# A pair's row sums one slot sooner, and one addition moved among four subtractions

## The chip, the cores and the metric

The kernel runs on one core of a Trainium2 chip. A core has five engines that run side by side, each with its own queue of instructions in a fixed order: TensorE (PE in the profile; its weight loads are listed as PEld), VectorE (DVE), ScalarE (ACT), GpSimd (POOL) and SyncE (SP), which here issues the DMA transfers. They meet through semaphores: an instruction that needs another engine's result waits at the head of its queue, and everything behind it waits too.

The metric is the time of one execution in device microseconds. Before the change it was 1029.43 us, the median of three runs (1029.31 to 1030.74).

## The reference

Two blocks follow each other. The first is block-sparse attention for a batch of 4, 8 heads, 768 tokens and head dimension 64:

```
scores = scale * q @ k.T
scores = where(mask, scores, -1e9)      # blocks of 32: window, first and last block, 3 sampled blocks
attn   = exp(scores - max) / (sum + 1e-9)
x      = attn @ v                       # -> (4, 768, 512)
```

The second mixes tokens and channels:

```
mixed = real(fft(fft(x, axis=1), axis=2))
u     = x + mixed
un    = (u - mean) / sqrt(var + 1e-6)
out   = u + relu(un @ w_ch1) @ w_ch2    # 512 -> 2048 -> 512
```

All of it is float32.

## The kernel before

**Pairs, units and slots.** Attention runs over 16 *pairs* of heads, four for each batch. A pair is cut in 12 *units* (two halves of the queries, six chunks of 128 keys each), and two units make a *slot*: six slots for a pair, 24 for a batch, 96 in all. For a unit, `scores` (L587) multiplies keys and queries on TensorE, ScalarE takes the exponential (L615), VectorE multiplies with the mask (L617), which gives the tile `e`, and `values` (L661) multiplies `e` with v on TensorE. Up to the first channel step (below) the mask is added on TensorE instead (L597) and the exponential writes `e` at once (L607). The flag `masks["by_pe"]` tells which; the first channel step makes it false for good, early in the third batch's attention.

**Row sums.** The softmax's denominators come from two steps. `gather` (L647) adds the tiles `e` of one half of a pair on GpSimd into `acc`, in two instructions a unit. When a pair is through, `total` (L746) lets TensorE sum `acc` over the partitions with a column of ones (`pick`), into the PSUM tile `sp`, and VectorE copies or adds that to `sums` (L714, L716). There are two buffers for `acc`, one for each half, so GpSimd cannot begin the next pair's `acc` before `total` has read the old one. `total` waits for GpSimd's last addition for the pair. Neither step issues a DMA.

**The mixer.** When a batch's attention is over, its second block begins while the next batch's attention goes on. `fourier` and the normalisation are a list of small steps (`apart`). The large products are *channel steps* (`late`): `quad` (L1133) computes hidden channels, `channels` (L1300, the tile `y`) the output, and L1305 adds `y` to `x` on VectorE. Both use a fast scheme of block matrix products with seven products for eight, which needs sums and differences of blocks first. The ones of the normalised input are made by `right` (L1087): four subtractions on VectorE, 128 x 768 elements each, called right sums in the prediction. `quad` starts with two products that need no right sum (the tiles `xp` and `yp`), then has three (the tile `z`) of which the first needs the second right sum. The right sums need the normalised input back from DRAM, where it was written and read again to be turned (`far<-un` and `unT<-far`). `xp`, `yp`, `y` and some others share two PSUM banks (the pool `ps_m`).

**Seams.** Where a batch's last channel steps end and the next batch's first `quad` begins, the order is: scores and values of a slot, the last two `y` products, then `xp`, `yp`, and the `z` that need the right sums. The right sums run on VectorE among the additions of the last `y`. There are three such seams with `right` of all three row tiles, for the mixers with `b` = 0, 1 and 2; the third of the four batches is `b` = 2. The seams of `b` = 1 and `b` = 2, called the second and the third batch's seam, lie at about 402 to 418 and 642 to 660 us. The row sums that fall in them are those of the first pair of the batch that follows the one a seam is named for.

**What sets the order.** The order on each engine is fixed when the program is built, by a planner in the kernel's own code. It keeps a planned clock for each engine (`when`), and every step has planned costs. Small steps wait in two lists. `short` holds matmul steps with the time from which they are ready, `apart` the mixer's steps. `gap` takes from `apart` as long as VectorE's planned work, with the step's own cost, does not run more than `rest + ahead` in front of TensorE's clock (2.0 + 2.2 us at a seam while a channel step is left, 2.0 + 3.0 after it), and then from `short` whatever is ready. In a slot that opens a pair (even number) nothing is taken once channel steps run, unless the slot opens a batch and all that is in `short` is ready. So `total` of a pair, put in `short` in the first slot of the next pair, is as a rule issued in its second slot, behind that slot's scores, and at the seams behind one `y` product more. The planner's costs of `right` are the last number in the entry's tuple (L1482). Which physical buffer or PSUM bank a tile gets is settled by the compiler at the build, not in this code.

```
if sl > SB and s == 0 and sl <= B * SB:
    short.append(("t", acc_at[n - 1, 1], lambda: total(n - 1)))
    state["total"] = short[-1]
```

`acc_at` is the planned time of GpSimd's last addition for the half.

Of the kernel before, what the change touches and what calls it, by code (L numbers as in the profile page):

```python
# [104 lines left out]
def kernel(  # L105
# [93 lines left out]
    when = {"PE": 0.0, "ACT": 0.0, "DVE": 0.0, "POOL": 0.0}  # L199
# [18 lines left out]
    def room(i, shape, name, dtype=FP32):  # L218
        return big.tile(shape, dtype, tag=f"big{i}", name=name)
# [276 lines left out]
    by_pe, to_gather = set(), deque()  # L496
    masks = {"by_pe": True}

    turned, e_of, acc_of, o_of, sums_of, x_of, sp_of = {}, {}, {}, {}, {}, {}, {}
    s_at, e_at, e_free, oT_at, acc_at = {}, {}, {}, {}, {}  # L500
# [237 lines left out]
    def total(n):  # L738

        b, j = pairs[n]  # L740
        sp, at = ps_t.tile([P, HS], FP32, tag="t", name="sp"), bank("t")
        for half in range(2):
            acc = acc_of.pop((n, half))
            for i in range(2):
                g = BLK * (2 * half + i)
                nc.tensor.matmul(sp[g:g + BLK, :], pick[:, BLK - j:2 * BLK - j], acc[:, i, :],  # L746
                                 start=True, stop=True, tile_position=(0, g))
        into_sums(b, j, sp)
        give(at, busy("DVE", 0.6, busy("PE", 0.7, acc_at[n, 1]) + HOP))
# [244 lines left out]
    def mixer(b, xA, xB):  # L994
# [69 lines left out]
        def spare_room():  # L1064
            if s:
                return
            rest, n, w = room(5, [P, ND * HS], "t4"), HS * ND // 2, P * ND // 2
            t[4] = rest[:, 0:n].rearrange("p (k n) -> p k n", n=HS)
            for i in (1, 3, 4):
                s[i] = rest[:, n:n + w].rearrange("p (k n) -> p k n", n=P)  # L1070
                n += w

        def right(j, *tiles):

            spare_room()
            if 1 not in t:
                both = room(4, [P, ND, HS], "t12")
                t[1], t[2], t[3] = both[:, K1, :], both[:, K2, :], unT[1][:, K1, :]
            b11, b21 = unT[0][:, K1, :], unT[0][:, K2, :]
            b12, b22 = unT[1][:, K1, :], unT[1][:, K2, :]  # L1080

            def part(ap):
                return ap.rearrange("p k (t n) -> p k t n", n=P)[:, :, tiles[0]:tiles[-1] + 1, :]

            to, a, c = {1: (t[1], b12, b11), 2: (t[2], b22, t[1]), 3: (b12, b22, b12),
                        4: (t[4], b21, t[2])}[j]
            tt(out=part(to), in0=part(a), in1=part(c), op=ALU.subtract)  # L1087
# [387 lines left out]
        if not last:  # L1475
            before = first + [pq[1], ar[0][1], ar[1][1], sp[0][1],
                              pq[2], wh[0][1], ft[0][1], ar[0][2], ar[1][2], sp[0][2],
                              pq[0], wh[0][2], ft[0][2], ar[0][0], ar[1][0], sp[0][0],
                              sp[1][1], wh[0][0], ft[0][0], sp[1][2], wh[1][1], ft[1][1],
                              sp[1][0], wh[1][2], ft[1][2], wh[1][0], ft[1][0]]  # L1480
            after = ([("-", un_back, 0.0, 0.0, 0.0)] + le +
                     [("b", lambda i=i: right(i, 0, 1, 2), 0.0, 0.0, 1.0 if b else 1.7)  # L1482
                      for i in (1, 2, 3, 4)])
        rest = []
        for r in range(2 if last else 0):
# [23 lines left out]
    short, apart, late, due = deque(), deque(), deque(), deque()  # L1509
# [89 lines left out]
    def begin(b):  # L1599


        before, after, rest = mixer(b, x_of[b, 0], x_of[b, 1])
        any_of = len(late) + len(apart) + 4 * len(rest)
        hold = 2 * T
        apart.extend((*step, any_of) for step in norm_steps(b) + before)
        apart.extend((*step, hold) for step in after)

        def go():
            late.extend(rest)
        apart.append(("-", go, 0.0, 0.0, 0.0, hold))  # L1610
# [21 lines left out]
    def slot(sl):  # L1632
        state["slot"] = sl
        phase, r = divmod(sl, SB)
        n, s = divmod(sl, SP)
# [56 lines left out]
        if s >= ((4 if late else 5) if reuse else 3) and (n, 0) in oT_at and once(n):  # L1692
            b, j = pairs[n]
# [13 lines left out]
        if sl < B * SB and n % NP == 1 and s == 1:  # L1707
            b = pairs[n - 1][0]
# [5 lines left out]
        if sl > SB and s == 0 and sl <= B * SB:  # L1714
            short.append(("t", acc_at[n - 1, 1], lambda: total(n - 1)))
            state["total"] = short[-1]
        if r == 0:
            needed.clear()
            needed.update(map(id, short))
# [79 lines left out]
    for sl in range(B * SB + 1):  # L1799
        slot(sl)  # L1800
        if sl == B * SB - 4:
            flag = highest()
        if sl == B * SB - 2:
            over = nc.values_load(flag[0:1, 0:1], min_val=0, max_val=1)
# [8 lines left out]
    def general():  # L1813
# [5 lines left out]
        for b in range(B):  # L1819
            xs = [xp.tile([P, T, DM], FP32, tag=tag, name="x") for tag in ("xA", "xB")]  # L1820
            for h in range(H):
# [43 lines left out]
                for half, x in enumerate(xs):  # L1865
                    sl = slice(half * T, half * T + T)
                    nc.vector.tensor_tensor(out=x[:, :, h * D:(h + 1) * D], in0=op[:, sl, :],
                                            in1=rs[:, sl, :].broadcast_to([P, T, D]),
                                            op=ALU.mult)
            before, after, rest = mixer(b, *xs)  # L1870
            for step in before + after:
                step[1]()
# [44 lines left out]
```

## Time and profile before

| what | value |
|---|---|
| median of three runs | 1029.43 us |
| the profiled execution | 1029.39 us |
| its span, first to last instruction | 1027.7 us |
| TensorE's granted clock in it | 0.999 of full |
| VectorE busy | 715.3 us |
| GpSimd busy | 330.0 us |

The profile gives for each engine the time in which it was busy. A row of the timeline tells when a run of equal instructions began, how long it took, on which engine and line, what it writes and reads, and how many there were. In brackets stands how long the engine was idle before it and whose work ended that. The list of waits sums these idle times. The chain follows the work that ended last backwards: at each step what released it.

TensorE's matmuls overlap a little, so the time between the starts of two rows tells more than one row's duration.

### The profile page before, as it was taken

To read this page: it belongs to the slowest core of one execution; us is meant where nothing else is said; L and a number is where in the kernel's file an instruction comes from. 1 tells how busy PE (TensorE), PEld (TensorE's weight loads), DVE (VectorE), ACT (ScalarE), POOL (GpSimd) and SP (SyncE) were. 2 spreads that over 40 slices of the span, in tenths; PEclk is the share of its full clock that TensorE was granted. 3 is DMA by queue.
4 is the path that set the end of the run, shared out by engine and by line. 5 is a ranking of instruction groups with operands and counts; after the bars stand their busy time and mean duration, and the time that the engine had idled before them with its cause. 6 is when DMAs were issued, how large, how long until landed. Compare 5 with 4: busy or idle time off the path is not lost.

```text
span 1027.7 us, 13038 instructions
## 1 busy us (share of the span) xinstructions
PE 1009.3 (98%) x4518; PEld 560.6 (55%) x4518; DVE 715.3 (70%) x1294; ACT 372.6 (36%) x763; POOL 330.0 (32%) x363
## 2 busy tenths in 40 slices
PE   8999999999999999999999999999999999999997
PEld 4434345444767764443444774444444765578576
DVE  6899895978984767755578577765458575675664
ACT  6998755553222222433440322343220321210210
POOL 1000183657634313554553232356550131000000
PEclk9999999999999999999999999999999999999999
DMA  7867422292000008432230003831010001200001
GB/s 216 228 188 228 116 48 47 52 144 37 1 1 1 11 10 158 92 69 40 55 61 1 1 11 78 153 56 43 16 24 8 0 2 50 43 1 0 1 13 53
DMA packets 182309, 60.46 MB, mean 59 GB/s; under 512 B 163018, under 2 KB 173012, under 8 KB 182236
## 3 DMA queue, kind: packets, MB, share of 16 engines
q1 hardware_dynamic: 181116, 58.95, 25.7%
q8 instruction: 38, 0.62, 0.3%
q10 hardware_dynamic: 1088, 0.59, 0.3%
q14 instruction: 35, 0.29, 0.1%
q0 software_dynamic: 32, 0.01, 0.0%
HBM read 46.14 MB, written 15.73 MB: 60 GB/s over the span
## 4 chain that ended last, share of the span: by engine, by line
PE 80%; DVE 10%; ACT 3%; DMA 3%; issue 2%; POOL 1%; SPq 1%; ACTq 0%; DVEq 0%; POOLq 0%
PE z L1133 16%; PE y L1300 13%; PE s L587 10%; PE o L661 9%; PE yp L1133 8%; PE yy L1396 7%; PE xp L1133 4%; PE yz L1241 3%; PE zp L869 2%; PE yc L1241 2%; PE yw L1241 1%; DVE x L939 1%; ACT e L607 1%; PE s L597 1%; PE sp L732 1%
## 5 line engine op out<-in xcount | busy, mean ns | idle before, releaser
L647 POOL TENSOR_TENSOR acc<-acc,e 128x384 f32<-128x384 f32 x160 | 165.5, 1068 | 88.5 <-DVE e L617 68.9
L587 PE MATMUL s<-qT,kT 64*128 64x384 f32 x768 | 153.7, 514 | 5.4 <-ACT e L607 3.7
L661 PE MATMUL o<-e,vr 128*64 128x384 f32 x768 | 142.2, 497 | 0.0
L617 DVE TENSOR_TENSOR e<-s,mask 128x768 f32<-128x768 f32 x86 | 78.2, 951 | 47.8 <-ACT s L615 39.7
L587 PEld LDWEIGHTS s<-qT,kT 64*128 64x128 f32 x768 | 63.7, 185 | 86.3 <-ACT e L607 23.1
L647 POOL TENSOR_TENSOR acc<-e 128x384 f32<-128x384 f32 x42 | 47.0, 1139 | 191.8 <-ACT e L607 121.2
L615 ACT ACTIVATE s<-s 128x768 f32<-128x768 f32 x86 | 65.2, 791 | 107.3 <-PE s L587 107.0
L607 ACT ACTIVATE e<-s 128x768 f32<-128x768 f32 x106 | 81.0, 812 | 53.8 <-PE s L597 32.5
L1133 PE MATMUL z<-unT,t 128*128 128x384 f32 x256 | 93.4, 488 | 0.9 <-DVE hA L1138 0.9
L661 PEld LDWEIGHTS o<-e,vr 128*64 128x64 f32 x768 | 47.7, 136 | 69.8 <-issue 68.5
L1138 DVE TENSOR_TENSOR hA<-z,hA 128x384 f32<-128x384 f32 x64 | 35.6, 557 | 63.5 <-PE z L1133 63.4
L1254 POOL TENSOR_TENSOR x<-of,x 128x256 f32<-128x256 f32 x45 | 39.2, 875 | 124.9 <-ACT of L1246 61.7
L1142 ACT ACTIVATE hA<-hA 128x384 f32<-128x384 f32 x64 | 33.5, 523 | 122.7 <-DVE hA L1138 122.7
L1300 PE MATMUL y<-w_sb,hB 128*128 128x512 f32 x168 | 75.4, 597 | 0.0
L1300 PE MATMUL y<-w_sb,hA 128*128 128x512 f32 x168 | 74.6, 596 | 0.0
L1133 PEld LDWEIGHTS z<-unT,t 128*128 128x128 f32 x256 | 48.3, 190 | 36.1 <-DVE hA L1138 3.3
L1142 ACT ACTIVATE hB<-hB 128x384 f32<-128x384 f32 x64 | 33.5, 523 | 85.9 <-DVE hB L1138 85.9
L1305 DVE TENSOR_TENSOR x<-y,x 128x512 f32<-128x512 f32 x42 | 29.0, 690 | 48.8 <-PE y L1300 48.7
L1300 PEld LDWEIGHTS y<-w_sb,hA 128*128 128x128 f32 x168 | 31.3, 190 | 39.8 <-issue 37.1
L1300 PEld LDWEIGHTS y<-w_sb,hB 128*128 128x128 f32 x168 | 30.9, 190 | 38.6 <-issue 38.6
L1153 ACT COPY hA<-xp 128x384 f32<-128x384 f32 x32 | 15.3, 477 | 92.3 <-PE xp L1133 89.9
L1133 PE MATMUL z<-t,w_sb 128*128 128x384 f32 x128 | 46.7, 487 | 1.5 <-DVE t L1087 1.5
(237 smaller groups left out, 1736.5 us busy)
## 6 DMA issues: line engine op xcount, KB each, us to landing
wraw<-in_moe_w_ch_dram SPq DMA_DIRECT2D x32, 512.0 KB
vr<-in_v_dram SPq DMA_DIRECT2D x30, 192.0 KB
far<-un SPq DMA_DIRECT2D x18, 256.0 KB
unT<-far SPq DMA_DIRECT2D x24, 192.0 KB
qb<-in_q_dram SPq DMA_DIRECT2D x44, 96.0 KB
kb<-in_k_dram SPq DMA_DIRECT2D x44, 96.0 KB
falls<-x SPq DMA_DIRECT2D x9, 256.0 KB
out_dram<-x SPq DMA_DIRECT2D x18, 128.0 KB
```

The costliest lines, as they stand in the source:

```text
L587: nc.tensor.matmul(s[:, i, 0:HS], kT[rows, c * P:(c + 1) * P], qT[rows, queries], start=True, stop=u not in by_pe)
L607: nc.scalar.activation(out=e, in_=s[:, :, 0:HS], func=ACT.Exp, scale=scale)
L615: nc.scalar.activation(out=s[:, :, 0:HS], in_=s[:, :, 0:HS], func=ACT.Exp, scale=scale)
L617: nc.vector.tensor_tensor(out=e, in0=s[:, :, 0:HS], in1=m.broadcast_to([P, 2, HS]), op=ALU.mult)
L647: nc.gpsimd.tensor_add(out=acc[:, i, :], in0=start[:, i, :], in1=e[:, i, :])
L661: nc.tensor.matmul(o[D * i:D * i + D, :], vt[:, i, c, :], e[:, i, :], start=(c == 0), stop=(c == C - 1))
L1133: nc.tensor.matmul(to, a[:, k, :], c[:, k, :], start=(k == 0), stop=(k == ND // 2 - 1))
L1142: nc.scalar.activation(out=h, in_=h, func=ACT.Relu)
L1241: nc.tensor.matmul(to, a[:, k, :], c[:, k, :], start=start and k == 0, stop=k == 1, skip_group_check=True)
L1254: nc.gpsimd.tensor_add(out=to, in0=kept[i], in1=to)
L1300: nc.tensor.matmul(y, hs[0, half][:, l, m * P:(m + 1) * P], w2_sb[:, 4 * r + l, :], start=(l == 0), stop=(l == 3))
L1396: nc.tensor.matmul(ps, a[:, k, :], c[k // 2][:, k % 2, :] if isinstance(c, list) else c[:, k, :], start=(k == 0), stop=(k == 3))
```

## The change

In the mixer's list, the planned cost of `right` for `b` = 1 goes from 1.0 to 1.2; for `b` = 0 and `b` = 2 it stays 1.7 and 1.0. In `slot`, once `masks["by_pe"]` is false, `total` is not left in `short`: it is issued at once, at the end of the pair's first slot, and the planner takes its input as ready then. Nothing is added to or taken from the work.

```diff
@@ -1479,7 +1479,7 @@
             after = ([("-", un_back, 0.0, 0.0, 0.0)] + le +
-                     [("b", lambda i=i: right(i, 0, 1, 2), 0.0, 0.0, 1.0 if b else 1.7)
+                     [("b", lambda i=i: right(i, 0, 1, 2), 0.0, 0.0, (1.7, 1.2, 1.0)[b])
                       for i in (1, 2, 3, 4)])
@@ -1714,6 +1714,9 @@
         if sl > SB and s == 0 and sl <= B * SB:
             short.append(("t", acc_at[n - 1, 1], lambda: total(n - 1)))
             state["total"] = short[-1]
+            if not masks["by_pe"]:
+                acc_at[n - 1, 1] = min(acc_at[n - 1, 1], when["PE"] - 0.2)
+                short.pop()[2]()
```

## The prediction

> **What bounds the kernel.** I read the page first, then the waits, then timelines of single engines around each pair's row sums (L746).
>
> ```profile
> span 1027.7 us, 13038 instructions
> PE 1009.3 (98%) x4518; PEld 560.6 (55%) x4518; DVE 715.3 (70%) x1294; ACT 372.6 (36%) x763; POOL 330.0 (32%) x363
> ```
>
> TensorE (PE) is busy for 1009.3 of 1027.7 us. The change takes no matmul away, so all it can win is part of the 18.4 us in which TensorE stands still. The profiled execution took 1029.39 us, 1.7 more than its span; the median of the three runs is 1029.43, so a sum against the one holds for the other. Less than 0.2% (2.06 us) could hardly be told from no change here.
>
> TensorE's own waits (us in total, times, longest; the last row from the answer for 665 us on), and the one of GpSimd (POOL) that the change is about:
>
> ```profile
> PE z L1133 <- DVE t L1087: 1.5, 1, 1.5
> ...
> PE yp L1133 <- ACT hA L1153: 0.6, 1, 0.6
> ...
> PE peak_row L1778 <- DVE peak L1776: 0.3, 1, 0.3
> ```
>
> ```profile
> POOL acc L647 <- PE sp L746: 66.5, 9, 9.9
> ```
>
> Nine times POOL cannot begin a new pair's additions because L746 has not yet read the old accumulator. By itself that costs nothing, for TensorE is busy meanwhile. The waits of 1.5 and 0.6 are what can be won; both lie at seams, where a batch's last products end while the next batch but one has its attention. From 665 us on the longest wait is 0.3.
>
> **The change, part by part.** The condition holds once a channel step has run, which is so for the last eight pair ends. Two of those, at the ends of the third and fourth batch, have their sums at once already; the row at 523.12 is one, and shows the order that the change brings. The row at 448.23 is one of the other six. (Timeline rows: start, duration, engine, line, count, and in brackets the idle time before and what ended it.)
>
> ```profile
> 446.74 1.56 PE L587 MATMUL s<-qT,kT 64*128 64x384 f32 x8
> 448.23 0.85 PE L746 MATMUL sp<-acc,pick 128*32 128x384 f32 x8
> ```
>
> ```profile
> 523.12 0.85 PE L746 MATMUL sp<-acc,pick 128*32 128x384 f32 x8
> 523.90 1.56 PE L587 MATMUL s<-qT,kT 64*128 64x384 f32 x8
> ```
>
> ```profile
> 435.42 3.87 POOL L647 TENSOR_TENSOR acc<-acc,e 128x384 f32<-128x384 f32 x4
> ```
>
> *Four moves at ordinary pair ends.* Scores take 448.23 − 446.74 = 1.49 and the sums 523.90 − 523.12 = 0.78. POOL is through at 439.29, 7.4 us before the sums' new place at 446.74, so TensorE does not wait, and two blocks change places: 0 us. The scores come 0.78 later, and so do ScalarE's exponentials and the mask multiplications of VectorE (DVE), whose results TensorE uses only behind the next product. The bounds are a loss and a gain of one 0.78 each; I take 0, as at 523 TensorE goes from the sums straight to the scores. The sums' addition on VectorE (L716) now stands in front of two mask multiplications, which wait for those same scores: 0. No DMA belongs to the sums, so SP's and POOL's queues keep their order.
>
> *The second batch's seam*, on TensorE, POOL and VectorE:
>
> ```profile
> 401.08 1.78 PE L587 MATMUL s<-qT,kT 64*128 64x384 f32 x8
> 402.79 3.70 PE L1300 MATMUL y<-w_sb,hB 128*128 128x512 f32 x8
> 406.42 0.85 PE L746 MATMUL sp<-acc,pick 128*32 128x384 f32 x8
> 407.20 3.70 PE L1300 MATMUL y<-w_sb,hB 128*128 128x512 f32 x8
> 410.74 1.45 PE L1133 MATMUL xp<-unT,w_sb 128*128 128x384 f32 x4
> 412.82 1.56 PE L1133 MATMUL yp<-unT,w_sb 128*128 128x384 f32 x4 [0.62 <-ACT hA L1153]
> ...
> 416.85 1.56 PE L1133 MATMUL z<-unT,t 128*128 128x384 f32 x4
> ```
>
> ```profile
> 396.60 3.86 POOL L647 TENSOR_TENSOR acc<-acc,e 128x384 f32<-128x384 f32 x4 [4.58 <-DVE e L617]
> 407.35 1.94 POOL L647 TENSOR_TENSOR acc<-e 128x384 f32<-128x384 f32 x2 [6.89 <-PE sp L746]
> 409.25 6.00 POOL L647 TENSOR_TENSOR acc<-acc,e 128x384 f32<-128x384 f32 x4
> ```
>
> ```profile
> 402.94 1.82 DVE L617 TENSOR_TENSOR e<-s,mask 128x768 f32<-128x768 f32 x2 [1.05 <-ACT s L615]
> ...
> 409.36 1.70 DVE L1087 TENSOR_TENSOR t<-unT 128x768 f32<-128x768 f32 x1 [2.14 <-DMA unT<-far]
> 411.09 1.64 DVE L1087 TENSOR_TENSOR t<-unT,t 128x768 f32<-128x768 f32 x1
> 412.65 1.75 DVE L1087 TENSOR_TENSOR unT<-unT 128x768 f32<-128x768 f32 x1
> ...
> 414.79 0.67 DVE L1305 TENSOR_TENSOR x<-y,x 128x512 f32<-128x512 f32 x1
> 415.39 0.94 DVE L1087 TENSOR_TENSOR t<-unT,t 128x768 f32<-128x768 f32 x1
> ```
>
> The sums go from 406.42 to 401.08. POOL's last addition for them ends at 400.46, so they need not wait. The scores behind them now find their two buffers free and take the 1.49 of the ordinary row instead of 402.79 − 401.08 = 1.71. So the first y starts at 401.08 + 0.78 + 1.49 = 403.35, the second as far behind it as now (406.42 − 402.79 = 3.63) at 406.98, and xp at 406.98 + (410.74 − 407.20) = 410.52: 0.22 sooner.
>
> POOL's six additions start near 402.0 instead of 407.35. Their last operand comes from the second mask multiplication, 0.78 later than now, at 404.76 + 0.78 = 405.5; at 1.0 us each they end by 408.6, before the first right sum (L1087) has its data at 409.36. That matters, because the four L1087 rows show two prices for one shape: 1.64 to 1.75 beside a busy POOL, 0.94 when POOL is through at 415.25. At the low price the first two are over at about 411.2 instead of 412.73.
>
> The planned cost of 1.2 moves the addition L1305. The planner lets VectorE's work run 2.0 + 2.2 = 4.2 us ahead of TensorE. The addition in front leaves VectorE 0.8 ahead and 0.1 is handing over, so by plan the third right sum ends at 0.8 + 0.1 + 3 × 1.0 = 3.9, and at 4.5 with 1.2 each: it is put off behind the last y product and that product's addition, which becomes the third operation, at 411.15 to 411.85. It frees a PSUM bank. The row of yp names ScalarE's copy of xp as what ended its wait, so yp sits in xp's bank today; the other bank was held to 415.46. The bank is settled when the program is built. Since the other will be free at 411.85, and xp's only at 412.82 − 0.22 = 412.60, I take the other: yp runs at 411.9 and the third z three products of 1.3 later, at 415.8 instead of 416.85: 1.1 gained. If yp stays in xp's bank, it is 0.25.
>
> *The third batch's seam.* Right sums and addition keep their order here; only the row sums move.
>
> ```profile
> 642.22 1.51 PE L661 MATMUL o<-e,vr 128*64 128x384 f32 x8
> 644.17 1.78 PE L587 MATMUL s<-qT,kT 64*128 64x384 f32 x8 [0.44 <-DVE e L617]
> ...
> 649.51 0.85 PE L746 MATMUL sp<-acc,pick 128*32 128x384 f32 x8
> ...
> 658.11 1.53 PE L1133 MATMUL z<-t,w_sb 128*128 128x384 f32 x4 [1.54 <-DVE t L1087]
> ```
>
> ```profile
> 639.04 4.47 POOL L647 TENSOR_TENSOR acc<-acc,e 128x384 f32<-128x384 f32 x4
> 650.44 2.19 POOL L647 TENSOR_TENSOR acc<-e 128x384 f32<-128x384 f32 x2 [6.93 <-PE sp L746]
> 652.59 4.56 POOL L647 TENSOR_TENSOR acc<-acc,e 128x384 f32<-128x384 f32 x4
> ```
>
> ```profile
> 646.03 1.82 DVE L617 TENSOR_TENSOR e<-s,mask 128x768 f32<-128x768 f32 x2 [1.05 <-ACT s L615]
> ...
> 654.03 0.69 DVE L1305 TENSOR_TENSOR x<-y,x 128x512 f32<-128x512 f32 x1 [1.79 <-PE y L1300]
> 654.64 1.66 DVE L1087 TENSOR_TENSOR t<-unT 128x768 f32<-128x768 f32 x1
> 656.34 1.63 DVE L1087 TENSOR_TENSOR t<-unT,t 128x768 f32<-128x768 f32 x1
> 657.89 0.95 DVE L1087 TENSOR_TENSOR unT<-unT 128x768 f32<-128x768 f32 x1
> ```
>
> ```profile
> 648.64 5.50 DMA unT<-far
> ```
>
> POOL ends at 643.51 and TensorE is free at 643.73, where it stands 0.44 for buffers: the sums fill that gap, and what follows comes about 0.7 sooner. That alone does not pay, because the z at 658.11 waits for the second right sum, whose data land at 654.14 (the last row, from the chain). What pays is POOL: freed at 643.73 + 0.78 = 644.5 instead of 650.4, with the mask multiplications of the next slot over by about 648, it ends its six additions near 651. The first right sum can start at 654.3 (today it stands behind the addition that ends at 654.72), the second ends two low prices later at 656.1, and z comes 0.14 behind, as now (658.11 against 657.97), at 656.26: 1.85 gained. The DMA itself is late next.
>
> From the rows, a right sum beside POOL costs 0.7 to 0.8 more than alone. The Trainium skill (SBUF — State Buffer, section Who interferes with whom) says that a VectorE instruction with two SBUF inputs and a GpSimd instruction that reads SBUF shut each other out for the whole instruction. By that rule a right sum would lose up to a whole POOL addition of 1.0, and freeing two of them would give about 0.5 more than I count; the measured rows decide.
>
> The sum: 1029.39 − 1.1 − 1.85 = 1026.4. It stays to the end, as TensorE has no longer wait left than 0.3.
>
> **The rivals.** *yp stays in xp's bank,* because the build ranks the banks otherwise or the addition does not move after all. For it: the margin is 0.75. Then 1029.39 − 0.25 − 1.85 = 1027.3.
>
> *The right sums stay slow,* because something other than POOL slows them. Then the second seam gives 0.25 and the third 654.64 − 654.3 = 0.35: 1028.8. Against it: at 657.89 a right sum takes 0.95 as soon as POOL's last addition (to 657.15) is over.
>
> *TensorE waits for POOL in the new place,* and the scores behind it too: the kernel is slower. The margin is 0.6 us in the second seam and 0.2 in the third; each microsecond beyond it costs one. To end 0.2% above before it must eat 2.95 and 2.06 more, 5.0 in two seams, so POOL must be 2.9 later at each. If the four additions in front take 1.75 each instead of about 1.0, what a right sum takes beside POOL, that is 3.0 later and 1031.6 us. For it: the third margin is thin, and the 6.00 row holds additions of 1.5. Against it: they run before anything that the change moves.
>
> **How the numbers follow.** The forecast 0.48, yp in xp's bank 0.26, right sums still slow 0.14, TensorE waiting for POOL 0.07; 0.05 is left for small shifts about these. Faster means under 1027.37: nearly all of the first case and half of the second, 0.61. Slower is 0.07, and the rest, 0.32, is no change that could be told. The range reaches up to the third case, and down to 1025.5, where the third seam keeps the 0.7 of the sums as well. The likeliest case alone spans 1025.8 to 1027.0.
>
> **What would show it.** The sums right behind L661 at both seams, without a wait for POOL; L1087 at 0.95 throughout; the addition third among them at the second seam, and yp without its 0.62; z at the third waiting under 0.6. It is wrong if L1087 still takes 1.6, or if the sums wait.

## The result and the profile after

The changed kernel takes 1027.81 us (median of 20 runs, 1026.02 to 1028.94); the kernel before, run beside it, 1029.47 (20 runs). The ratio of the two, by the means of these runs, is 0.9978 with a 95% interval of 0.9972 to 0.9985: 2.3 us faster, within 1.5 to 2.9 (the two medians lie 1.66 apart). The profiled execution took 1027.32 us, 2.07 less than the one before. It is a small gain, a little above what can be told from none. The forecast was 1026.4; the first rival, yp in xp's bank, was given 1027.3.

The page's head and TensorE's waits, of the kernel after (us in total, times, longest):

```profile
span 1025.6 us, 13037 instructions
PE 1008.2 (98%) x4518; PEld 560.5 (55%) x4518; DVE 712.4 (69%) x1294; ACT 372.7 (36%) x763; POOL 327.2 (32%) x363
```

```profile
PE z L1133 <- DVE t L1087: 0.9, 1, 0.9
```

VectorE is busy 2.9 us less: by their rows the eight right sums of the two seams fell from 11.2 to 7.6 us in all, and the rest of VectorE's work took some 0.6 longer. The z's wait went from 1.5 to 0.9; yp's 0.62 is untouched (its row below). The second batch's seam, on TensorE, GpSimd and VectorE:

```profile
400.86 0.85 PE L746 MATMUL sp<-acc,pick 128*32 128x384 f32 x8
401.85 1.78 PE L587 MATMUL s<-qT,kT 64*128 64x384 f32 x8
403.56 7.13 PE L1300 MATMUL y<-w_sb,hB 128*128 128x512 f32 x16
...
412.61 1.56 PE L1133 MATMUL yp<-unT,w_sb 128*128 128x384 f32 x4 [0.62 <-ACT hA L1153]
```

```profile
404.81 3.86 POOL L647 TENSOR_TENSOR acc<-acc,e 128x384 f32<-128x384 f32 x4
```

```profile
410.41 0.96 DVE L1087 TENSOR_TENSOR t<-unT 128x768 f32<-128x768 f32 x1 [2.42 <-DMA unT<-far]
411.40 0.96 DVE L1087 TENSOR_TENSOR t<-unT,t 128x768 f32<-128x768 f32 x1
412.28 0.68 DVE L1305 TENSOR_TENSOR x<-y,x 128x512 f32<-128x512 f32 x1
```

GpSimd is through at 408.67 and the right sums take 0.96, as forecast. But yp still waits 0.62 for ScalarE's copy of xp: it stayed in xp's bank. And the data of the right sums came at 410.41 and not at 409.36. No product waits for them at this seam: the first z begins 1.39 behind yp, as before the change (414.00 − 412.61, 414.21 − 412.82). The third batch's seam:

```profile
641.84 1.51 PE L661 MATMUL o<-e,vr 128*64 128x384 f32 x8
643.28 0.85 PE L746 MATMUL sp<-acc,pick 128*32 128x384 f32 x8
644.06 1.56 PE L587 MATMUL s<-qT,kT 64*128 64x384 f32 x8
...
656.15 1.53 PE L1133 MATMUL z<-t,w_sb 128*128 128x384 f32 x4 [0.89 <-DVE t L1087]
```

```profile
654.05 0.96 DVE L1087 TENSOR_TENSOR t<-unT 128x768 f32<-128x768 f32 x1 [0.64 <-DMA falls<-x]
```

The sums fill the old gap, the right sums take 0.96, and the first one now waits 0.64 for a DMA. The row names `falls<-x`, a transfer that shares no tile with the right sums in the kernel and was issued right behind the last `unT<-far`. I take it that they wait for `unT<-far`, their data; the row does not show it.

To see what each seam gave, take the start of the values (L661) ahead of it and behind it. In the kernel before, then after:

```profile
399.57 1.51 PE L661 MATMUL o<-e,vr 128*64 128x384 f32 x8
...
422.49 2.16 PE L661 MATMUL o<-e,vr 128*64 128x384 f32 x12
...
666.30 2.16 PE L661 MATMUL o<-e,vr 128*64 128x384 f32 x12
```

```profile
399.42 1.51 PE L661 MATMUL o<-e,vr 128*64 128x384 f32 x8
...
422.11 2.48 PE L661 MATMUL o<-e,vr 128*64 128x384 f32 x14
...
664.34 2.80 PE L661 MATMUL o<-e,vr 128*64 128x384 f32 x16
```

The second seam took 422.49 − 399.57 = 22.92 before and 22.69 after: 0.23 won. The third took 666.30 − 642.22 = 24.08 before and 664.34 − 641.84 = 22.50 after: 1.58 won. Between the seams every block of values is 0.38 earlier than before, at 427 as at 567, so the ordinary pair ends give 0.00. 0.15 was there at 399 already, ahead of everything that the change touches, and about 0.1 came at 737, where the wait for `peak` fell from 0.3 to 0.2. So 0.15 + 0.23 + 1.58 + 0.1 = 2.06 of the 2.07.

### The profile page after: what moved, and what is told of

It reads as the page before. It is cut to its first block, busy times and chain, and to the rows that moved or that the text cites. A ratio compares the mean times of both kernels' runs of the same rounds, so it can differ in the third digit from the quotient of the medians.

```text
span 1025.6 us, 13037 instructions
## 1 busy us (share of the span) xinstructions
PE 1008.2 (98%) x4518; PEld 560.5 (55%) x4518; DVE 712.4 (69%) x1294; ACT 372.7 (36%) x763; POOL 327.2 (32%) x363
## 4 chain that ended last, share of the span: by engine, by line
PE 84%; DVE 9%; ACT 3%; issue 2%; DMA 2%; SPq 0%; POOL 0%; ACTq 0%; DVEq 0%; POOLq 0%
PE z L1133 16%; PE y L1300 14%; PE s L587 11%; PE o L661 10%; PE yp L1133 8%; PE yy L1396 7%; PE xp L1133 4%; PE yz L1241 3%; PE yc L1241 2%; PE zp L869 2%; PE yw L1241 2%; PE sp L732 1%; DVE x L939 1%; PE s L597 1%; ACT e L607 1%
## 5 line engine op out<-in xcount | busy, mean ns | idle before, releaser
L647 POOL TENSOR_TENSOR acc<-acc,e 128x384 f32<-128x384 f32 x160 | 162.6, 1051 | 105.2 <-DVE e L617 85.6
L661 PE MATMUL o<-e,vr 128*64 128x384 f32 x768 | 142.2, 497 | 0.0
L661 PEld LDWEIGHTS o<-e,vr 128*64 128x64 f32 x768 | 47.7, 136 | 69.8 <-issue 68.5
```

What stands on the lines that cost most here:

```text
L647: nc.gpsimd.tensor_add(out=acc[:, i, :], in0=start[:, i, :], in1=e[:, i, :])
L661: nc.tensor.matmul(o[D * i:D * i + D, :], vt[:, i, c, :], e[:, i, :], start=(c == 0), stop=(c == C - 1))
```

## The experiments

The same two differences were taken for every run, from the rows, which are rounded to 0.01. Negative is time won against the kernel before, in us; where a seam is not changed in a run, it is a control for how much a seam varies by itself. Eight of these kernels were executed once only (all but the changed kernel, sums_12 and first_split), so what they show is read from the seams and not from their time. The rows under each run are of its timeline.

| run | second seam | third seam |
|---|---|---|
| the changed kernel | −0.23 | −1.58 |
| the changed kernel again | −0.06 | −1.42 |
| cost_only | +0.11 | +0.01 |
| sums_8 | −0.66 | 0.00 (control) |
| sums_12 | +0.06 (control) | −2.19 |
| pool_filler | −0.65 | −1.70 |
| filler_seams | −0.65 | +0.17 |
| yp_other | −0.84 | −1.69 |
| add_1st | −1.15 | −1.63 |
| split_b2 | −0.65 | −2.00 |
| pool_late | −0.44 | −0.27 |
| first_split | −1.16 | −2.09 |

**One part alone: the row sums of the third seam.** The kernel before, with the change's new lines under a condition for one pair only; the planned cost stays 1.0.

```diff
-            if not masks["by_pe"]:
+            if n - 1 == 12:
```

> The kernel before, with the row sums taken early at the end of one pair alone, the one in the third batch's seam (pair 12); the planned cost stays 1.0. My theory: the third seam's gain stands by itself, because it comes from GpSimd being through before the right sums begin. Right sums 0.96 each there, the z waits about 0.9 instead of 1.54, TensorE comes out of the seam 1.6 us sooner than in the kernel before, and the run is 1.6 to 1.7 us faster (about 1027.8 where the kernel before shows 1029.4). Rival: the gain at this seam needs the second seam to have moved too (through the transfers, which are ordered in one queue); then the seam gives under 1.0. Rival: the right sums are slow for another reason than GpSimd; then they stay at 1.6 and the seam gives 0.35.

The seam gave 2.19, more than in the whole change, and the z waited 0.27. The right sums took 0.96 and the first began right behind the addition (654.25 to 654.94) with no wait for data; it stands 11.61 behind the values, for 12.21 in the changed kernel, and this 0.60 is nearly all of the difference between the two gains (0.61). TensorE and VectorE in the third seam:

```profile
657.06 1.53 PE L1133 MATMUL z<-t,w_sb 128*128 128x384 f32 x4 [0.27 <-DVE t L1087]
```

```profile
654.97 0.96 DVE L1087 TENSOR_TENSOR t<-unT 128x768 f32<-128x768 f32 x1
```

So the gain needs nothing of the second seam. The time of the whole run (1028.57 us in the median, ratio 0.9988, 0.9979 to 0.9998) shows less than the seam, 1.2 us; its profile, too, had lost 1.24 us at 238 to 250 us, far ahead of the change (last section).

**One part alone: the planned cost.**

```diff
-  ... right(i, 0, 1, 2), 0.0, 0.0, 1.0 if b else 1.7)
+  ... right(i, 0, 1, 2), 0.0, 0.0, (1.7, 1.2, 1.0)[b])
```

> The kernel before, with the planned cost 1.2 alone; no row sums are moved. My theory: nothing is won, since yp waits for ScalarE's copy of xp and not for the addition: yp begins at 412.8 with its wait of 0.62, as before. The two first right sums still take 1.6 to 1.7 beside GpSimd, the copy of the sums and the addition then stand in front of the third, the fourth ends near 416.5 and the third z, which stands behind an addition on VectorE after it, comes 0.2 later: 0 to +0.2 us. Rival (the prediction's): the addition's place decides yp's bank; then yp's wait changes with the addition, which here ends near 414, so yp would begin near 414 and the kernel be 1.2 us slower.

VectorE and TensorE in the second seam:

```profile
411.94 1.63 DVE L1087 TENSOR_TENSOR t<-unT,t 128x768 f32<-128x768 f32 x1
...
413.96 0.67 DVE L1305 TENSOR_TENSOR x<-y,x 128x512 f32<-128x512 f32 x1
414.56 1.64 DVE L1087 TENSOR_TENSOR unT<-unT 128x768 f32<-128x768 f32 x1
```

```profile
413.66 1.56 PE L1133 MATMUL yp<-unT,w_sb 128*128 128x384 f32 x4 [0.62 <-ACT hA L1153]
```

The addition moved and yp did not: it begins at 413.66, before the addition ends at 414.63. The seam cost 0.11. The addition's place in front of the third sum did not change yp's bank.

**One part alone: the row sums of the second seam.** As sums_12, with `n - 1 == 8`.

> The kernel before, with the row sums early at the pair in the second batch's seam (pair 8) alone, planned cost 1.0, so the addition stays fourth. My theory: yp keeps its wait of 0.62, the right sums take 0.96, and TensorE comes out of the seam 0.2 us sooner; the planned cost has no part in that. Third seam as in the kernel before (z waits 1.5). Total -0.2. Rival (the prediction's): without the addition in third place less is won than with it, so 0 or a loss, and in the whole change the addition gave the 0.2.

The diff is that of sums_12 but for the pair. 0.66 was won with the addition still fourth, the same as in three later runs with the addition third (0.65). The planned cost of 1.2 is worth nothing here. By the starts of TensorE's rows the 0.66 has four parts: 0.07 between the values and what follows them, 0.22 in the scores (1.49 up to the y products, for 1.71 before), 0.20 in the two y products that are now back to back, and 0.17 behind yp, around the third z, which in the kernel before stood behind VectorE's late right sums. My 0.2 was too low, since it was read from the first profile of the changed kernel, where the scores came late (see its second profile below).

**What slows the right sums.** Filler on GpSimd. A first attempt put it behind units 99 and 147, one pair too early:

> The changed kernel with filler for GpSimd behind its six additions of both seams: in the second batch's seam twelve memsets of 128x384 (they write SBUF and read nothing), in the third's nine additions of two accumulator halves, as the real ones are; both write the accumulator of the half that has not begun yet, so the result is the same. Theory that the right sums are slowed by GpSimd's reads: beside the memsets they stay at 0.96 and the second seam is unchanged; beside the additions they take 1.63 to 1.75, the z of the third seam waits 2.2 to 2.4 instead of 0.89, and the run is 1.3 to 1.5 us slower than the changed kernel. By the Trainium skill's rule (SBUF — State Buffer, Who interferes with whom) of whole instructions that shut each other out, memsets would not matter either, and a right sum beside additions would take up to 1.95: z 0.5 later still. Theory that any busy GpSimd slows VectorE: 1.6 or more at both seams. Theory that something else slowed the right sums before: 0.96 at both, no change.

Neither seam saw filler, so the run says nothing of its theories. It serves as one more profile of both seams as the change has them (−0.65 and −1.70). The filler itself cost 2.9 us at 238 to 250 us and 2.5 at 540 to 568, where TensorE soon needs what GpSimd and VectorE do. The second attempt is one pair later:

```diff
+def _filler(nc, acc_p, acc_of, n, u):
+    if u not in (111, 159):
+        return
+    acc = acc_of[n, 0]
+    to = acc_of[n, 1] = acc_p.tile([128, 2, 384], FP32, tag="acc", name="acc")
+    for i in range(9 if u == 159 else 12):
+        if u == 159:
+            nc.gpsimd.tensor_add(out=to[:, i % 2, :], in0=acc[:, 0, :], in1=acc[:, 1, :])
+        else:
+            nc.gpsimd.memset(to[:, i % 2, :], 0.0)
```

> The changed kernel with the filler one pair later than in the run before, so that it stands where it was meant to: on GpSimd behind the six additions of each seam, twelve memsets in the second batch's seam, nine additions in the third's. Theory that the right sums are slowed by GpSimd's reads: beside the memsets they stay at 0.96 each; beside the additions they take 1.63 to 1.75, the z of the third seam waits 1.4 longer than without filler (2.2 to 2.4 instead of 0.8 to 0.9), and TensorE leaves that seam with 0.2 instead of 1.6 us gained on the kernel before. By whole instructions that shut each other out a right sum could take up to 1.95, 0.3 more each. Theory that any busy GpSimd slows VectorE: 1.6 or more at both seams. Theory that something else slowed the right sums before: 0.96 at both and 1.6 gained.

In the second seam memsets run from 408.21 to 412.60, in the third additions from 650.34 on (L1895 and L1893 are the filler's lines). GpSimd, VectorE and TensorE:

```profile
408.21 4.39 POOL L1895 MEMSET acc<- 128x384 f32 x12
...
650.34 10.78 POOL L1893 TENSOR_TENSOR acc<-acc 128x384 f32<-128x384 f32 x8
```

```profile
410.32 0.96 DVE L1087 TENSOR_TENSOR t<-unT,t 128x768 f32<-128x768 f32 x1
...
654.34 1.63 DVE L1087 TENSOR_TENSOR t<-unT,t 128x768 f32<-128x768 f32 x1
655.89 1.75 DVE L1087 TENSOR_TENSOR unT<-unT 128x768 f32<-128x768 f32 x1
```

```profile
656.12 1.53 PE L1133 MATMUL z<-t,w_sb 128*128 128x384 f32 x4 [1.47 <-DVE t L1087]
...
659.83 1.56 PE L1133 MATMUL z<-unT,t 128*128 128x384 f32 x4 [0.90 <-DVE hA L1138]
```

Beside memsets a right sum takes 0.96, beside additions 1.63 to 1.75, and the whole gain of the third seam is gone (+0.17 for −1.4 to −1.7). GpSimd's additions were the cause, not GpSimd being busy, and the rival that something else slows the right sums is out. Memsets and additions stood in different seams, but in the kernel before both seams had slow right sums beside additions. The size of the z's first wait was 1.47, not 2.2 to 2.4: the first right sum came 0.4 earlier behind the values than in yp_other (below) and was slowed for part of its length only (1.36); the rest was lost at the third z, which stands behind the slow third and fourth sums on VectorE. The Trainium skill (SBUF — State Buffer, Who interferes with whom) has it that a GpSimd instruction which only writes SBUF does not get in the way of a VectorE instruction with two inputs, and the memsets agree. By its lock for the whole instruction a pair would take, as an estimate from the rows of each alone, 0.96 + 1.00 = 1.96; the 1.63 to 1.75 here are less.

**yp in the other bank.** Every tile of `ps_m` keeps the bank that the build gave it, except for this yp.

```diff
-    ps_m = ctx.enter_context(tc.tile_pool(name="ps_m", bufs=2, space=PSUM))
+    ps_m = _Banks(ctx, tc)   # two pools of one buffer; a list names the bank of each tile
```

> The changed kernel with every tile of the pool ps_m put into the bank that it has there, but for yp of the second batch's seam, which goes into the other bank (the last y's). The prediction's step: the addition stands third on VectorE, is over 0.65 to 0.75 before ScalarE's copy of xp, and yp begins 0.6 to 0.7 sooner than in xp's bank; TensorE leaves the seam that much sooner. My theory now: in the changed kernel's trace that addition ended at 412.96 and the copy at 412.55, since the right sums began at 410.41 with the data's landing and not at 409.36; so yp begins 0.3 to 0.4 later than in xp's bank and nothing is won: yp waits 0.9 to 1.0 for the addition instead of 0.62 for the copy, and the seam costs 0.3 more.

TensorE and VectorE in the second seam:

```profile
410.10 1.45 PE L1133 MATMUL xp<-unT,w_sb 128*128 128x384 f32 x4
411.98 1.56 PE L1133 MATMUL yp<-unT,w_sb 128*128 128x384 f32 x4 [0.43 <-DVE x L1305]
```

```profile
409.38 0.96 DVE L1087 TENSOR_TENSOR t<-unT 128x768 f32<-128x768 f32 x1 [1.82 <-DMA unT<-far]
...
411.25 0.68 DVE L1305 TENSOR_TENSOR x<-y,x 128x512 f32<-128x512 f32 x1
```

Neither figure held. This time the data came at 409.38, as before the change, and the addition ended at 411.93, almost where the prediction had put it (411.85); yp began at 411.98. But xp ended at 411.55, sooner than forecast, so the copy too would have freed its bank sooner. The wait fell from 0.62 to 0.43, and the seam gave 0.84 for 0.65: the other bank is worth 0.19, not 0.7.

**The addition in front of all right sums.**

```diff
+ ... held.append(lambda: right(i, 0, 1, 2)) if b == 1 and i < 3 else right(i, 0, 1, 2) ...
             nc.vector.tensor_tensor(out=x[:, m, :], in0=y, in1=x[:, m, :], op=ALU.add)
+            [f() for f in held]; held.clear()
```

> The changed kernel with the addition of the second batch's seam in front of all four right sums instead of in front of the third. The build then puts yp into the other bank. My theory: the addition follows the last y at once and is over 0.5 before xp is, so yp runs right behind xp without a wait; the right sums begin with the data as before or 0.7 later, the second is through 0.2 before yp ends or just then, and the seam gives 0.5 to 0.65 more than in the changed kernel with equal landing of the data. Rival: the right sums stand one addition later and the first z waits for them what yp no longer waits: 0.

VectorE and TensorE in the second seam:

```profile
410.39 0.69 DVE L1305 TENSOR_TENSOR x<-y,x 128x512 f32<-128x512 f32 x1 [2.74 <-PE y L1300]
...
411.98 0.96 DVE L1087 TENSOR_TENSOR t<-unT,t 128x768 f32<-128x768 f32 x1
```

```profile
411.48 1.45 PE L1133 MATMUL yp<-unT,w_sb 128*128 128x384 f32 x4
413.08 1.53 PE L1133 MATMUL z<-t,w_sb 128*128 128x384 f32 x4 [0.15 <-DVE t L1087]
```

The build now chose the other bank by itself (yp begins at 411.48, before ScalarE's copy of xp at 411.73), and yp's 0.62 is gone; the z pays 0.15 of it back. The seam gave 1.15: 0.50 over the 0.65.

**Right sums in halves.** In the third seam, first halves of the first two, then second halves.

```diff
-  for i in (1, 2, 3, 4)
+  for i, k in ((1, (0, 1)), (2, (0, 1)), (1, (1, 2)), (2, (1, 2)), (3, 0), (4, 0)) if b == 2
```

> The changed kernel with the first two right sums of the third batch's seam cut in halves by the product's two steps of its inner dimension: first halves of both, then second halves. My theory: the z waits for the data and for the two right sums behind it, nothing else. With halves of 0.5 to 0.55 the z's first step needs only two of them: its wait goes from 0.89 to about 0.15 (its second step waits 0.3 then), and the seam gives 0.4 to 0.6 more, or all of the wait where the data land earlier. Rival: the product waits for whole tiles, not halves; then four halves with their start-up take 0.2 longer than two wholes and the seam loses 0.2.

TensorE in the third seam:

```profile
654.26 1.88 PE L1133 MATMUL z<-t,w_sb 128*128 128x384 f32 x4
655.98 1.45 PE L1133 MATMUL z<-t,t 128*128 128x384 f32 x4
```

The z has no wait ahead of it, but takes 1.72 from its start to the next one's, for 1.37 in the changed kernel: its second step waits inside. The seam gave 2.00 for the 1.58 to 1.70 of the same seam with whole right sums, but not all of that is the halves: the first right sum also began 11.97 behind the values, for 12.10 to 12.21. From the first right sum's start to the next values it is 10.11 here, for 10.28 to 10.29 in yp_other, add_1st and the changed kernel: the halves are worth 0.17 or 0.18, not the 0.4 to 0.6 expected, for the third sum begins 2.13 behind the first half (655.10 − 652.97) where it began 1.87 behind the first whole (655.92 − 654.05).

**GpSimd late for the row sums.** This is the rival that ends slower, priced.

```diff
+ [nc.gpsimd.tensor_tensor(out=acc[:, 1, :], in0=acc[:, 1, :], in1=e[:, 1, :], op=op)
+  for op in ((ALU.add, ALU.subtract) if u == 155 else ())]
```

> The changed kernel with two instructions more on GpSimd as the last ones ahead of the row sums of the third batch's seam: they add the last unit's e to half of the accumulator and take it away again (1.0 us each). The sums then wait for GpSimd, about 1.8. By the prediction's price, one for one: the seam gives 1.8 less than the changed kernel's 1.6, so nothing or a loss of 0.2 against the kernel before. My theory: the z behind it waits 0.8 to 0.9 for the data anyway, and these do not depend on the sums; so only 1.8 - 0.85, about 0.95, is lost and the seam still gives 0.6 to 0.7; the z's wait is gone.

TensorE in the third seam (L648 is one of the two added instructions):

```profile
645.22 0.83 PE L746 MATMUL sp<-acc,pick 128*32 128x384 f32 x2 [1.21 <-POOL acc L648]
645.98 1.56 PE L587 MATMUL s<-qT,kT 64*128 64x384 f32 x8
...
657.34 1.53 PE L1133 MATMUL z<-t,w_sb 128*128 128x384 f32 x4 [0.15 <-DVE t L1087]
```

The values began at 641.72 here, so the scores came 645.98 − 641.72 = 4.26 behind them, for 644.06 − 641.84 = 2.22 in the changed kernel: 2.04 late. The z's wait fell from 0.89 to 0.15 and took up 0.74; the seam gave 1.31 less, which is 2.04 less 0.74. So the price is not one for one: the wait for the data is a cushion.

**The changed kernel again, and the best of both.**

> The changed kernel once more, for a second profile of it. My theory: in its first profile the data of the second seam came 1 us late because one DMA issue on SP took 1.89 us at 391.3 (0.6 elsewhere), and the seam gave 0.22; with the issue on time, as in four profiles of kernels that leave this seam as it is, it gives 0.65, the third 1.6 to 1.7, 0.1 later on: 2.35 to 2.45 under the kernel before. Rival: the 0.22 belongs to the changed kernel (its instructions are those of the first profile), so 0.22 again and 2.0 to 2.1 in all.

> The changed kernel with both edits that won in the runs before: in the second batch's seam the addition in front of the right sums, and in the second and the third batch's seam the first two right sums cut in halves. My theory adds up what the single runs showed on TensorE: second seam 1.15 (addition first) plus the 0.15 that the z still waited there, third seam 2.0, 0.1 later on: 3.4 under the kernel before in the profile, and 1.0 to 1.2 under the changed kernel where its data are on time. Rival: the halves cost VectorE in the second seam what they save, so 3.2. Rival: the transfers eat it (the data land when they land, whatever stands ahead): then no better than the changed kernel, 2.3 under the kernel before.

The second profile of the changed kernel gave 0.06 and 1.42; 1027.63 us (11 runs), ratio 0.9972 (0.9963 to 0.9981). So 0.65 is not what this kernel shows as a rule. The right sums' data are late again (410.54), but that is not what costs, since no product waits for them. It is the scores. The chain of the first profile, then ScalarE's row of the same copy in sums_8:

```profile
395.83 2.71 DMA out_dram<-x
...
398.79 0.04 ACT x L685
...
400.83 0.97 DVE e L617
...
401.85 1.78 PE s L587 x8
```

```profile
398.22 0.48 ACT L685 COPY x<-xt 128x384 f32<-128x384 f32 x1 [3.08 <-PE y L1300]
```

L685 copies attention's result into a buffer of `x` that an output transfer must have read first, and ScalarE's exponential, VectorE's mask and the scores stand behind it. In the first profile the scores begin 0.21 later behind the sums than in sums_8 and take 1.71 as before the change, so 0.07 − 0.21 + 0.20 + 0.17 = 0.23; in the second they begin 0.37 later, which leaves 0.07 of the same sum for a measured 0.06. The copy begins 1.36 ahead of the values in sums_8, 0.84 in pool_late, 0.63 and 0.47 in the two profiles of the changed kernel, and the seam gives 0.66, 0.44, 0.23 and 0.06.

What these late profiles share is a row on SP's queue (SPq, the DMA issues) ahead of the seam. In sums_8, then in the changed kernel again:

```profile
391.47 0.60 SPq L1042 DMA_DIRECT2D unT<-far  x1
```

```profile
391.30 1.97 SPq L1042 DMA_DIRECT2D unT<-far  x1
```

Where this issue took 0.60 (sums_8, both filler runs, split_b2), the seam with the row sums moved gave 0.65 or 0.66; where it took 1.45 to 1.97 (pool_late, both profiles of the changed kernel), 0.06 to 0.44. The output transfers are issued behind it on the same queue. But for pool_filler's memsets these kernels issue the same instructions in the same order up to there. What settles it from run to run was not found, nor that nothing else differs.

first_split, with the addition first and the halves in both seams, took 1026.00 us (5 runs, 1025.86 to 1027.44), ratio 0.9963 (0.9949 to 0.9976), with 1.16 and 2.09 won in the seams. That is 1.6 us below the changed kernel's median in the same comparison, with intervals that overlap; it beats the kernel before clearly. In its waits neither yp nor the z of the seams appears any longer.

## Why the prediction was right, and where it was not

The direction, the range and the order of size held: faster by 0.22%, 1027.8 between 1025.5 and the third case's 1028.8. The likeliest case did not happen; the first rival did, at 1027.3 for a profiled 1027.32 and a median of 1027.81. That the profile hits it so closely is luck: the terms were 0.25 and 1.85 and measured 0.23 and 1.58, with 0.25 from elsewhere; and the 0.23 is not made of what the 0.25 was, for the scores' 0.22 did not come in that profile. Two of the signs that the prediction named failed: yp kept its 0.62, and the z of the third seam waited 0.89 and not under 0.6.

- *Ordinary pair ends, 0:* right. The values stand 0.38 earlier at 427 and at 567 alike.
- *The right sums at the low price in both seams:* right, and the cause shown by filler_seams. The eight sums took 3.6 us less in all.
- *Scores 0.22 shorter in the second seam:* right where ScalarE's copy of x was on time: sums_8 has their row at 1.56 for 1.78. Another 0.44 of that seam the prediction did not count: 0.20 in the two y products, now back to back, 0.17 behind yp and 0.07 ahead of the sums. In both profiles of the changed kernel the scores kept 1.78 and began 0.21 and 0.37 late, behind that copy.
- ***"Since the other will be free at 411.85 … I take the other":*** this step failed, and with it the term of 1.1. The build kept yp in xp's bank; the addition's place before the third sum did not change that (cost_only), its place before the first did (add_1st). The bank's share of that term, 1.1 − 0.25 = 0.85, was also too large: with the other bank and data on time it measured 0.19, because the copy's bank comes free earlier as well; the whole seam then gave 0.84. Only the addition in front of all right sums wins the wait, 0.50 of 0.62.
- *The third seam, 1.85:* right in mechanism, measured 1.58, 1.42 and 1.63 to 1.70 with the same instructions there. Of the 0.27 missing in the first profile 0.13 is the data, which let the first right sum begin 12.21 behind the values where 654.3 − 642.22 = 12.08 was counted; 0.14 is the two sums with their handing over, 2.10 (656.15 − 654.05) where 1.96 was counted (its 656.1 left 1.8 for two sums that take 0.95 each). The forecast that the DMA is late next was right, and the data's time is what scatters: 11.6 to 12.4 behind the values over the runs.
- *TensorE waiting for GpSimd:* it did not; the margin was 643.28 − 643.12 = 0.16 in the third seam and 0.55 in the second. The price, one for one, was wrong: the z's wait takes up the first 0.74.
- *"SP's and POOL's queues keep their order":* true, and not enough. The order was kept; the moment was not, and by way of ScalarE's copy the second seam's gain hung on it.

## What to carry to other kernels

When a step is moved, ask of the wait to be won which buffer it hangs on, and who chose that buffer: a release that comes sooner wins nothing if the build has tied the waiter to another one. A seam's gain is bounded by the transfer that is late next, and that transfer's time scatters from run to run: the second seam of one kernel gave 0.23 and 0.06 for the 0.65 of others. Several profiles, compared at the same instruction, tell the parts apart where medians can't. Before a late transfer is blamed, follow the chain: the one that was seen late first, the right sums' data, cost nothing at that seam. And look for GpSimd's reads in a window in which VectorE has two-input work: keeping them out took the right sums beside them from 1.63 to 1.75 down to 0.96 each.

## What was not expected of the hardware

Who comes first decides who pays. At 231 us, far ahead of the change, a right sum and GpSimd's second addition begin almost together. In the kernel before, the addition had begun; in sums_12 the right sum came first. GpSimd's and VectorE's rows of the kernel before, then GpSimd's, VectorE's and TensorE's of sums_12:

```profile
230.50 3.64 POOL L647 TENSOR_TENSOR acc<-acc,e 128x384 f32<-128x384 f32 x3 [3.53 <-DVE acc L642]
```

```profile
231.53 1.74 DVE L1087 TENSOR_TENSOR t<-unT 128x768 f32<-128x768 f32 x1 [0.71 <-DMA unT<-far]
```

```profile
230.35 4.37 POOL L647 TENSOR_TENSOR acc<-acc,e 128x384 f32<-128x384 f32 x3 [3.53 <-DVE acc L642]
```

```profile
231.23 0.96 DVE L1087 TENSOR_TENSOR t<-unT 128x768 f32<-128x768 f32 x1 [0.56 <-issue]
```

```profile
237.29 0.92 PE L587 MATMUL s<-qT,kT 64*128 64x384 f32 x4 [0.62 <-ACT e L607]
```

There the right sum takes 0.96 and three additions 4.37 for 3.64. GpSimd, 0.7 later, holds up ScalarE, ScalarE the scores (0.62), and TensorE comes out at 250 us 1.24 later. cost_only shows the same, 1.2; the other kernels with these instructions do not, apart from pool_filler, whose filler stood there. A start that differs by 0.15 relative to GpSimd's thus costs half as much as the whole change wins. The Trainium skill (SBUF — State Buffer, Who interferes with whom) says that the order of issue decides who blocks, and these rows agree. It is a likely part of why runs of one kernel differ by 2 us and more, which was not tested by itself.
